# First product of a second MLP: seven products of 256 columns in place of eight, and an integer rounding

## The chip, the cores and the metric

The kernel runs on one core of a Trainium2 chip. The metric is the device time of one execution in microseconds (us). The engines are PE (matrix products), DVE, ACT and POOL (element work), and SP, which issues DMAs.

## What is computed

Attention in two stages over 8 batches of 576 positions, 8 heads of 64, gives x of 4608 rows and 512 columns. Two MLPs follow; the change concerns the second one.

```python
def _moe_ref(x, w_in, w_out):          # first MLP: 512 -> 2048 -> 512
    h = x @ w_in
    g = h * (1.0 / (1.0 + np.exp(-h)))
    return (g @ w_out).astype(np.float32)

def _moe2_ref(x, w_in, w_out):         # second MLP, same sizes
    h = x @ w_in
    g = h * np.cos(h)
    return (g @ w_out).astype(np.float32)
```

The weights arrive as 64-bit floats and are decoded in the kernel.

## The kernel before

Every operation is recorded by a planner (`Plan`, from line 81) together with what it reads and writes. The planner prices each one (`price`), works out due times backwards, simulates a list schedule several times, and then issues the operations in the order of the best schedule; so each engine has one fixed order, written down in advance, and all instructions carry the line at which the planner wraps a call, L196. `plan.due` sets a due time by hand, `plan.release` an earliest time. For PSUM, `region` (line 115) returns the whole bank, so operations on different columns of a bank are ordered one after the other. Operations recorded within `plan.either()` go to whichever of two engines the schedule finds first: `copy` to ACT or DVE, `combine` to DVE or POOL. `split(d, x)` (line 518) makes two parts of an fp32 tile, the rounded value and the rest, and `mm3` (line 502) multiplies split operands with three matmuls.

The first MLP runs over 256 steps (`first`, line 847) of 288 token columns and 128 of the 2048 hidden units: 6 matmuls into a bank of `hb`, then ACT, DVE and POOL work, then 12 into the four banks `acc`. Four pairs of batches follow each other, and the attention of the next pair runs between the steps. Results go to DRAM (`ydram`, and `ypart` for the first pair, which is computed in four parts). During the last pair, released at 380 us of the planner's time, `w2_unit` (line 565) prepares the second MLP's weights: load into one of two buffers `wd`, decode by way of `wy`, split into the same `wd`, store to `w2dram`; 32 units.

`change(top, [att], ...)` (line 1064) then closes the pool that holds attention's and the decoding's tiles and opens the tiles for y in its place, so y can be loaded once all of that is done. The second MLP goes over 9 blocks of 512 tokens and, in each, 16 chunks of 128 hidden units: 144 steps of `second` (line 923). A step is 12 matmuls of 512 columns into one of four banks in turn (`sb`, `mb`, `hb0`, `hb1`), then h x cos(h), then 12 matmuls of 512 columns into `acc`, due three steps later (`LAG`). The rounding of h/2pi is done by adding a large constant (`ROUND`) on ACT and subtracting it on DVE. All weights of the second MLP are loaded once and stay in `W`; `load_y` (line 905) loads and splits a block's input one block ahead, into two sets of buffers.

The functions that the change touches:

Of the kernel before, what the change touches and what calls it, by code (L numbers as in the profile page):

```python
# [25 lines left out]
ROUND = 12582912.0  # L26
# [54 lines left out]
class Plan:  # L81
# [73 lines left out]
    def price(self, engine, f, out, ins):  # L155
# [11 lines left out]
        if engine == self.DVE:  # L167
            fast = sbuf and f in ("tensor_copy", "tensor_scalar", "memset") and m == n
            if f == "scalar_tensor_tensor" and sbuf and ins[0].dtype == F32:
                return 67 + n / 0.53, 0  # L170
            return 67 + max(m, n) / (1.92 if fast else 0.96), 0
# [216 lines left out]
def attention_mlps_kernel(  # L388
# [24 lines left out]
    TB = 512  # L413
    NBLK = NT // TB
# [50 lines left out]
    w2dram = dram.tile([FC, 2, P, 2, 512], F32, name="w2dram")  # L465
# [13 lines left out]
    def late(name, dtype):  # L479

        return Late(name, W[0] if dtype == F32R else f32(W[0][:, 0]))
# [20 lines left out]
    def mm3(dst, lhs, rhs, first, last):  # L502

        T.matmul(dst, lhs[1], rhs[0], start=first, stop=False)
        T.matmul(dst, lhs[0], rhs[1], start=False, stop=False)
        T.matmul(dst, lhs[0], rhs[0], start=False, stop=last)
# [19 lines left out]
    late_wy = tiles(att, [P, WIDE], I32, "wy", 2)  # L526
# [38 lines left out]
    def w2_unit(c, i):  # L565
        if i == 0:
            src = w_in2[:, 2 * c * P : 2 * (c + 1) * P].rearrange("(k p) f -> p k f", p=P)
        else:
            src = w_out2[c * P : (c + 1) * P]
        DMA.dma_start(w2dram[c, i], f32(decode_parts(src)))  # L570

# [275 lines left out]
    def first(s):  # L847
# [28 lines left out]
        if end:  # L876
            t0 = pr * 2 * S + k0
# [9 lines left out]
    NS2 = NBLK * FC  # L887
    order = list(range(3, NBLK)) + [0, 1, 2]
    win, wout = {}, {}
    yt = {}  # L890
    banks = [sb, mb, hb[0], hb[1]]

    def lates(name, dtype, n):
        ts = [late(f"{name}{i}", dtype) for i in range(n)]
        return ts, ring(ts)

    ysts, yst = lates("yst", F32, 1)
    yads, yad = lates("yad", F32, 1)
    ys, yring = lates("y", F32R, 2 * KC)
    ns, nring = lates("n", F32, 2)  # L900
# [4 lines left out]
    def load_y(i, c):  # L905

        t0 = order[i] * TB
        st = yst()
        DMA.dma_start(st, ydram[c, :, t0 : t0 + TB])
        n = min(TB, 2 * S - t0)  # L910
        for part in ypart if n > 0 else ():
            ad = yad()
            DMA.dma_start(ad[:, :n], part[c, :, t0 : t0 + n])
            combine(st[:, :n], st[:, :n], ad[:, :n], ALU.add)
        yt[i, c] = yring()
        split(yt[i, c], st)

    def load_w2(c, base):
        win[c], wout[c] = W[base[0]], W[base[1]]
        DMA.dma_start(f32(win[c]), w2dram[c, 0])  # L920
        DMA.dma_start(f32(wout[c]), w2dram[c, 1])

    def second(s):

        i, fc = divmod(s, FC)
        h = banks[s % 4]
        w = win[fc]
        plan.due = due_second(s)
        for kc in range(KC):
            c = slice(kc * P, kc * P + P)  # L930
            y = yt[i, kc]
            mm3(h, (w[:, 0, c], w[:, 1, c]), (y[:, 0], y[:, 1]), kc == 0, kc == KC - 1)
        plan.due = None
# [12 lines left out]
        w = wout[fc]  # L946
        for t in range(4):
            plan.due = due_second(s + LAG)
            c = slice(t * P, t * P + P)
            mm3(acc[t], (g[:, 0, c], g[:, 1, c]), (w[:, 0], w[:, 1]), fc == 0, fc == FC - 1)  # L950
            plan.due = None
            if fc == FC - 1:
# [5 lines left out]
                r0 = order[i] * TB + t * P  # L958
                DMA.dma_start(out[r0 : r0 + P, :], o)
# [6 lines left out]
    def due_second(s):  # L966
        return due_first(NS) + 5540 * s
# [70 lines left out]
    for pr in range(NPAIR):  # L1038
# [25 lines left out]
    change(top, [att], "yp", "right", ysts + yads + ys)  # L1064
    change(mid, [a2p], "cp", "left", ns + rs_ + g2s + os_)
    for c in range(KC):
        load_y(0, c)
    for c in range(FC):
        if c < 4:
            load_w2(c, (FC + 2 * c, FC + 2 * c + 1))  # L1070
        elif c < 8:
            load_w2(c, (FC + 4 + c, FC + 8 + c))
        else:
            load_w2(c, (2 * (c - 8), 2 * (c - 8) + 1))
    for s in range(NS2):
        i, fc = divmod(s, FC)
        if fc == 0 and i + 1 < NBLK:
            for c in range(KC):
                load_y(i + 1, c)
        second(s)  # L1080
# [28 lines left out]
```

## Time and profile before

| | us |
|---|---|
| median of 3 runs | 1580.67 (1580.16 to 1581.14) |
| span of the profiled execution | 1579.2 |
| PE busy | 1554.3 |
| DVE / ACT / POOL busy | 1101.2 / 783.5 / 200.2 |
| DMA, mean over the span | 99 GB/s |

The profiled execution is one more run; its span goes from its first to its last instruction and is 1.5 us under the median of the timed runs. A record of PE lasts longer than the slot that the matmul takes, since matmuls are pipelined: rates are read from starts and counts, not from the mean length. PEld is the loading of the weights of a matmul.

### The profile page before, as it was taken

The page shows a single profiled execution, that of the slowest core. Times are in us where ns is not written, and L with a number is a line of the kernel's source. Part 1 is how long each engine was busy: PE and PEld are TensorE (multiplying, and loading weights), DVE is VectorE, ACT ScalarE, POOL GpSimd, SP SyncE. Part 2 cuts the span into 40 slices and gives each one's busy share as a digit, 9 for nine tenths or more (in the row PEclk, how much of TensorE's full clock was granted, in tenths as well). Part 3 has the DMA queues.
Part 4 walks back from the last instruction along what each step waited for, and adds up shares of the span by engine and source line. Part 5 has one row for each costly group of instructions (what it writes and reads, how often), then busy time and mean ns, then how long its engine had stood idle before and what let it go on. Part 6 is the DMA issues. An engine that isn't in the chain of part 4 may idle for free.

```text
span 1579.2 us, 26881 instructions
## 1 busy us (share of the span) xinstructions
PE 1554.3 (98%) x10344; PEld 1339.1 (85%) x10344; DVE 1101.2 (70%) x2031; ACT 783.5 (50%) x1549; POOL 200.2 (13%) x189
## 2 busy tenths in 40 slices
PE   9889999999999999999999999999999999999999
PEld 7678888999789988899988888888888888888887
DVE  5897666465787879775366767676766878676665
ACT  5876545344455565644344544444444444444443
POOL 0221111010112112120000010000100112121111
PEclk9899999999999999999999999999999999999999
DMA  9667475122775677552720101010010303010000
GB/s 248 178 221 206 124 151 136 51 46 51 165 230 184 182 175 195 193 196 83 257 99 7 47 1 54 1 54 1 27 48 20 95 19 94 21 61 0 20 9 27
DMA packets 217665, 156.96 MB, mean 99 GB/s; under 512 B 154048, under 2 KB 182720, under 8 KB 217536
## 3 DMA queue, kind: packets, MB, share of 16 engines
q1 hardware_dynamic: 217536, 155.24, 34.1%
q8 instruction: 81, 1.33, 0.4%
q14 instruction: 48, 0.39, 0.1%
HBM read 108.27 MB, written 46.92 MB: 98 GB/s over the span
## 4 chain that ended last, share of the span: by engine, by line
PE 86%; DVE 9%; DMA 2%; ACT 1%; issue 1%; SPq 0%; POOL 0%; DVEq 0%; ACTq 0%; POOLq 0%
PE acc L196 45%; PE hb L196 23%; PE sb L196 9%; PE mb L196 9%; DVE wy L196 2%; DVE big L196 1%; DVE w L196 1%; DVE wd L196 1%; DVE gf L196 1%; DMA wd<-in_moe_w_out 1%; DVE wde L196 1%; DVE rsb L196 1%; DVE g L196 0%; SPq L196 0%; DMA w2dram<-wd 0%
## 5 line engine op out<-in xcount | busy, mean ns | idle before, releaser
L196 PE MATMUL acc<-g,w 128*128 128x288 f32 x3072 | 470.1, 298 | 2.8 <-ACT ysb L196 2.1
L196 PE MATMUL acc<-w,g 128*128 128x512 f32 x1728 | 464.0, 389 | 0.8 <-DVE o L196 0.8
L196 PEld LDWEIGHTS acc<-g,w 128*128 128x128 f32 x3072 | 425.8, 188 | 28.9 <-issue 19.9
L196 PEld LDWEIGHTS acc<-w,g 128*128 128x128 f32 x1728 | 324.1, 188 | 69.2 <-DVE o L196 1.5
L196 PE MATMUL hb<-a,w 128*128 128x288 f32 x1536 | 263.8, 301 | 7.1 <-ACT a L196 2.9
L196 PEld LDWEIGHTS hb<-a,w 128*128 128x128 f32 x1536 | 222.6, 190 | 30.1 <-issue 14.9
L196 ACT ACTIVATE r<-r 128x512 f32<-128x512 f32 x144 | 91.0, 632 | 315.9 <-DVE r L196 315.5
L196 PE MATMUL hb<-y,w 128*128 128x512 f32 x864 | 239.2, 389 | 0.0
L196 PEld LDWEIGHTS hb<-y,w 128*128 128x128 f32 x864 | 162.1, 188 | 33.6
L196 ACT CAST g<-gf 128x288 fp32r<-128x288 f32 x223 | 96.2, 432 | 159.2 <-PE acc L196 125.6
L196 DVE SCALAR_TENSOR_TENSOR gf<-gf,hb 128x288 f32<-128x288 f32 x256 | 114.0, 447 | 55.0 <-ACT gf L196 53.6
L196 POOL TENSOR_TENSOR g<-gf,g 128x288 fp32r<-128x288 f32 x89 | 86.3, 970 | 508.2 <-ACT g L196 428.4
L196 ACT ACTIVATE gf<-hb 128x288 f32<-128x288 f32 x256 | 104.5, 411 | 87.9 <-PE hb L196 77.5
L196 DVE TENSOR_TENSOR g<-gf,g 128x288 fp32r<-128x288 f32 x167 | 78.1, 469 | 98.7 <-ACT g L196 97.1
L196 POOL TENSOR_TENSOR g<-r,g 128x512 fp32r<-128x512 f32 x44 | 57.1, 1298 | 591.1 <-ACT g L196 586.3
L196 DVE SCALAR_TENSOR_TENSOR r<-n,r 128x512 f32<-128x512 f32 x144 | 125.5, 871 | 2.8
L196 PE MATMUL sb<-y,w 128*128 128x512 f32 x432 | 121.6, 389 | 0.0
L196 PE MATMUL mb<-y,w 128*128 128x512 f32 x432 | 120.9, 389 | 0.0
L196 ACT ACTIVATE r<-r,half_pi 128x512 f32<-128x512 f32 x144 | 104.1, 723 | 4.1
L196 DVE TENSOR_TENSOR r<-r,hb 128x512 f32<-128x512 f32 x72 | 49.5, 687 | 74.9 <-ACT r L196 74.5
L196 PEld LDWEIGHTS mb<-y,w 128*128 128x128 f32 x432 | 80.9, 188 | 16.7
L196 PEld LDWEIGHTS sb<-y,w 128*128 128x128 f32 x432 | 81.0, 188 | 16.6
(189 smaller groups left out, 1576.4 us busy)
## 6 DMA issues: line engine op xcount, KB each, us to landing
w2dram<-wd SPq DMA_DIRECT2D x32, 512.0 KB, 3.3
w<-w2dram SPq DMA_DIRECT2D x32, 512.0 KB, 4.5
wd<-in_moe_w_in SPq DMA_DIRECT2D x24, 512.0 KB, 4.4
w<-w1dram SPq DMA_DIRECT2D x48, 256.0 KB, 3.4
wd<-in_moe_w_out SPq DMA_DIRECT2D x20, 512.0 KB, 4.2
ydram<-ysb SPq DMA_DIRECT2D x64, 144.0 KB, 2.2
yst<-ydram SPq DMA_DIRECT2D x36, 256.0 KB, 2.6
out<-o SPq DMA_DIRECT2D x36, 256.0 KB, 2.1
```

The source lines that it names most:

```text
L196: run = lambda: emit(*[real(x) for x in args], **{k: real(x) for k, x in kw.items()})
```

## The change

The first product of the second MLP is computed with Strassen's scheme: the two halves of a batch's tokens and the two halves of the 512 inputs and of the 2048 hidden units make a 2x2 by 2x2 product, for which seven products of combined operands stand in place of eight. A block is now 256 tokens of either half of the batches (columns t of `ydram` are rearranged to that end), a step covers two chunks of hidden units, `fp` and `fp + 8`, and there are 72 steps. A product is 2 chunks of inputs x 3 matmuls of 256 columns. It is accumulated in halves of two banks, X (`hb`) and Y (`mb`, `sb`), alternating by step; between the products two ACT copies and two DVE sums carry partial results from one half to another. The combined weights are made beforehand (`win2_unit`), stored in `w2s` and loaded anew for every block, 256 KB for each product, into a ring of 16 buffers; those of product 0 stay. The combined inputs are made in `load_y` (products 0 to 2) and during the last step of the block before (products 3 to 6). The second product is as before, with other due times. The rounding is done by letting ACT write 32-bit integers. A third buffer `wy` is added. One branch of the planner's price now looks at the last operand's type.

The core of the diff:

```diff
-    TB = 512
-    NBLK = NT // TB
+    TB = 256
+    NBLK = NT // (2 * TB)
+    FH = FC // 2
-    w2dram = dram.tile([FC, 2, P, 2, 512], F32, name="w2dram")
+    w2dram = dram.tile([FC, P, 2, 512], F32, name="w2dram")
+    w2s = dram.tile([2, 7, P, 4, 2, 2, P], F32, name="w2s")
-    late_wy = tiles(att, [P, WIDE], I32, "wy", 2)
+    late_wy = tiles(att, [P, WIDE], I32, "wy", 3)
+    def wout2_unit(c):
+        DMA.dma_start(w2dram[c], f32(decode_parts(w_out2[c * P : (c + 1) * P])))
+    def win2_unit(F, c):
+        def block(y, i, j):
+            f = (FH * i + 4 * F) * P
+            decode(w_in2[(c + 2 * j) * P : (c + 2 * j + 1) * P, 2 * f : 2 * (f + 4 * P)], y)
+        def put(y, prod):
+            flat = rings["wd"]().rearrange("p f t -> p (f t)")
+            d = flat.bitcast(F32R).rearrange("p (q t f) -> p t q f", q=4, t=2)
+            split(d, y.bitcast(F32).rearrange("p (q f) -> p q f", q=4))
+            DMA.dma_start(w2s[F, prod, :, :, c].rearrange("p q t f -> p q (t f)"), flat.bitcast(F32).rearrange("p (q x) -> p q x", q=4))
+        y = [rings["wy"]() for _ in range(3)]
+        v = [x.bitcast(F32) for x in y]
+        block(y[0], 1, 0)
+        block(y[1], 1, 1)
+        combine(v[2], v[0], v[1], ALU.add)
+        put(y[1], 6)
+        block(y[1], 0, 0)
+        put(y[1], 0)
+        put(y[2], 1)
+        combine(v[2], v[2], v[1], ALU.subtract)
+        combine(v[0], v[1], v[0], ALU.subtract)
+        put(y[2], 2)
+        put(y[0], 4)
+        block(y[1], 0, 1)
+        put(y[1], 3)
+        combine(v[1], v[1], v[2], ALU.subtract)
+        put(y[1], 5)
-    banks = [sb, mb, hb[0], hb[1]]
+    X, Y = hb, [mb, sb]
+    raws, raw = lates("raw", F32, 10, TB)
+    ys, _ = lates("y", F32R, 12, TB)
+    yring = ring(ys + [as_y(x) for x in halves[0:2] + halves[26:32]])
+    held = halves[2:4] + halves[20:26]
+    uring = ring(halves[4:16] + halves[16:20])
+    AHEAD_Y = 3
         n = nring()
-        A.activation(n, h, AF.Copy, scale=INV_2PI / WEIGHT, bias=ROUND)
-        V.tensor_scalar(n, n, ROUND, None, op0=ALU.subtract)
+        A.activation(n, h, AF.Copy, scale=INV_2PI / WEIGHT)
-            plan.due = due_second(s + LAG)
+            plan.due = due_second(s + (2.1 if fc >= FH else 1.6))
+    def second(s):
+        i, fp = divmod(s, FH)
+        x, y = X[s % 2], Y[s % 2]
+        x1, x2, y1, y2 = x[:, :TB], x[:, TB:], y[:, :TB], y[:, TB:]
+        ws = [held[fp]] + [uring() for _ in range(6)]
+        ws = [as_w(ws[0]) if i else load_unit(ws[0], fp, 0)] + [load_unit(w, fp, j) for j, w in enumerate(ws) if j]
+        def product(prod, dst, start, due):
+            plan.due = due_second(s + due)
+            for c in range(2):
+                b = yt[i, prod, c]
+                w = ws[prod]
+                mm3(dst, (w[:, c, 0], w[:, c, 1]), (b[:, 0], b[:, 1]), start and c == 0, c == 1, skip_group_check=True)
+            plan.due = None
+            if fp == FH - 1 and i + 1 < NBLK and prod + AHEAD_Y < 7:
+                later[i + 1](prod + AHEAD_Y)
+        m5 = m5ring()
+        product(0, x1, True, 0)
+        product(1, x2, False, 0.1)
+        A.copy(y1, x1)
+        A.copy(m5, x2)
+        product(2, y1, False, 0.35)
+        product(3, x1, False, 0.45)
+        V.tensor_tensor(x2, y1, m5, ALU.add)
+        product(4, y1, False, 0.6)
+        product(5, x2, False, 0.7)
+        V.tensor_tensor(y2, y1, m5, ALU.add)
+        half_second(s, fp, x)
+        product(6, y1, False, 0.95)
+        half_second(s, fp + FH, y)
-        return due_first(NS) + 5540 * s
+        return due_first(NS) + 10480 * s
-            for c in range(FC):
-                for i in range(2):
-                    w2_unit(c, i)
+            for F in range(2):
+                for c in range(2):
+                    win2_unit(F, c)
+                for c in range(4 * F, 4 * F + 4):
+                    wout2_unit(c)
+                    wout2_unit(c + FH)
-    change(top, [att], "yp", "right", ysts + yads + ys)
+    change(top, [att], "yp", "right", raws + yads + m5s + ys)
+    load_y(0)
+    for prod in range(AHEAD_Y, 7):
+        later[0](prod)
```

## Rows read from the trace of the kernel before

**Rows 1.** The page's part 1: busy us, share of the span, instructions, for PE.

```profile
PE 1554.3 (98%) x10344; PEld 1339.1 (85%) x10344; DVE 1101.2 (70%) x2031; ACT 783.5 (50%) x1549; POOL 200.2 (13%) x189
```

**Rows 2.** Busy time by stretch: PE, PEld, DVE, ACT, POOL (count), granted clock, DMA share, GB/s.

```profile
560.00:720.00 160.00, 157.42 (x1377) 141.34 (x1376) 123.70 (x244) 88.69 (x204) 26.74 (x26) 1.00 0.65 191
720.00:800.00 80.00, 80.00 (x575) 78.19 (x574) 36.91 (x81) 32.05 (x69) 0.81 (x1) 1.00 0.55 178
800.00:1560.00 760.00, 759.23 (x3348) 627.75 (x3347) 537.33 (x892) 348.60 (x564) 90.15 (x75) 1.00 0.10 32
```

**Rows 3.** The chain that ended last: start, length, what.

```profile
820.13 2.27 PE hb L196 x10
841.89 2.27 PE hb L196 x10
```

**Rows 4.** Busy time by stretch, where PE runs 288-column matmuls alone.

```profile
720.00:780.00 60.00, 60.00 (x455) 60.00 (x454) 28.27 (x64) 23.34 (x53) 0.81 (x1) 1.00 0.48 156
```

**Rows 5.** Instructions in order of time, PEld: start, length, engine, operation, count.

```profile
555.38 0.30 PEld L196 LDWEIGHTS acc<-g,w 128*128 128x128 f32 x2
...
555.75 0.19 PEld L196 LDWEIGHTS acc<-g,w 128*128 128x128 f32 x1
```

**Rows 6.** Groups by shape, 800 to 1560 us: count, busy us, mean ns, idle before.

```profile
L196 DVE SCALAR_TENSOR_TENSOR r<-n,r 128x512 f32<-128x512 f32 x141 | 123.4, 875 | 2.7
...
L196 ACT ACTIVATE r<-r,half_pi 128x512 f32<-128x512 f32 x141 | 102.0, 723 | 4.1
L196 ACT ACTIVATE r<-r 128x512 f32<-128x512 f32 x140 | 88.5, 632 | 309.5 <-DVE r L196 309.0
...
L196 DVE TENSOR_TENSOR g<-r,g 128x512 fp32r<-128x512 f32 x97 | 68.4, 705 | 2.2
L196 ACT CAST g<-r 128x512 fp32r<-128x512 f32 x104 | 64.4, 620 | 28.6 <-DVE r L196 26.7 <-POOL yst L196 1.6
L196 DVE TENSOR_SCALAR n<-n 128x512 f32<-128x512 f32 x140 | 63.0, 450 | 32.6 <-ACT n L196 32.4
L196 DVE TENSOR_SCALAR r<-r 128x512 f32<-128x512 f32 x140 | 60.4, 431 | 4.1
...
L196 DVE SCALAR_TENSOR_TENSOR r<-n,hb 128x512 f32<-128x512 f32 x71 | 48.8, 687 | 3.5
...
L196 ACT ACTIVATE n<-hb 128x512 f32<-128x512 f32 x71 | 42.2, 594 | 25.9 <-PE hb L196 25.5
```

**Rows 7.** The page's part 5 and its longer view: 288-column operations on DVE and ACT.

```profile
L196 DVE TENSOR_TENSOR g<-gf,g 128x288 fp32r<-128x288 f32 x167 | 78.1, 469 | 98.7 <-ACT g L196 97.1
...
L196 ACT ACTIVATE ysb<-acc 128x288 f32<-128x288 f32 x107 | 41.4, 411 | 24.4 <-PE acc L196 16.5 <-DMA ypart<-ysb 5.7 <-DMA ydram<-ysb 1.8
```

**Rows 8.** A 256 KB load (KB, us to landing), and the busiest DMA stretch.

```profile
w<-w1dram SPq DMA_DIRECT2D x48, 256.0 KB, 3.4
...
760.00:800.00 40.00, 40.00 (x273) 38.19 (x272) 16.48 (x35) 15.88 (x33) 0.00 (x0) 1.00 0.80 269
```

**Rows 9.** Tile `wd`, 410 to 710: ns min/median/max, first and last start; DMA to landing.

```profile
L196 ACT ACTIVATE wd<-wd x32: 659/675/697, 419.5 to 690.1; 128x512 int32<-128x512 uint32 x32
...
L196 DVE SCALAR_TENSOR_TENSOR wy<-wy,wd x32: 673/692/1640, 422.0 to 695.1; 128x512 int32<-128x512 int32 x32
...
L196 SPq DMA_DIRECT2D w2dram<-wd x32: 319/326/1448, 427.7 to 700.7; - x32
...
w2dram<-wd SPq DMA_DIRECT2D x32, 512.0 KB, 3.3
...
wd<-in_moe_w_in SPq DMA_DIRECT2D x24, 512.0 KB, 4.4
```

**Rows 10.** Tile `yst` 700 to 760, and PE in order of time.

```profile
L196 SPq DMA_DIRECT2D yst<-ydram x9: 319/320/427, 708.0 to 748.8; - x9
...
783.38 0.39 PE L196 MATMUL sb<-y,w 128*128 128x512 f32 x1
```

**Rows 11.** PE in order of time at the end.

```profile
1561.75 13.54 PE L196 MATMUL acc<-w,g 128*128 128x512 f32 x59
```

More of the change, by code (lines that the diff above doesn't have):

```diff
@@ L25 @@
 TWO_PI_LO = 2.0 * math.pi - 6.28125
-ROUND = 12582912.0
 DOWN = 2.0**-111
@@ L500, in attention_mlps_kernel, with mm3 @@
     pbds = [const.tile([P, H // 2, 2 * NP], F32, name=f"pbd{i}") for i in range(2)]
[L502 to L506, printed above, removed]
+    def mm3(dst, lhs, rhs, first, last, **kw):
+        T.matmul(dst, lhs[1], rhs[0], start=first, stop=False, **kw)
+        T.matmul(dst, lhs[0], rhs[1], start=False, stop=False, **kw)
+        T.matmul(dst, lhs[0], rhs[0], start=False, stop=last, **kw)
     def copy(dst, src):
@@ L876, in first @@
         if end:
-            t0 = pr * 2 * S + k0
+            t0 = k0 // HALF % 2 * (2 * S if part else NT) // 2 + (2 * pr + k0 // S) * HALF
             dst = ypart[part - 1] if part else ydram
@@ L903, in attention_mlps_kernel @@
     os_, oring = lates("o", F32, 2)
-    def load_y(i, c):
-        t0 = order[i] * TB
[L908 to L933, printed above, removed]
+    halves = [W[FC + kc * 4 + s][:, i] for s in range(4) for kc in range(2) for i in range(2)]
+    halves += [W[FC + 8 + kc * 4 + s][:, i] for s in range(4) for kc in range(2) for i in range(2)]
@@ new lines, in attention_mlps_kernel, with load_y, load, put @@
+    as_y = lambda x: x.rearrange("p (t n) -> p t n", t=2)
+    as_w = lambda x: x.rearrange("p (k t f) -> p k t f", k=2, t=2)
+    yring = ring(ys + [as_y(x) for x in halves[0:2] + halves[26:32]])
+    held = halves[2:4] + halves[20:26]
+    uring = ring(halves[4:16] + halves[16:20])
+    AHEAD_Y = 3
+    later = {}
+    def load_y(i):
+        t0 = order[i] * TB
+        n = min(TB, S - t0)
+        def load(kc, h):
+            st = raw()
+            DMA.dma_start(st, ydram[kc, :, h * NT // 2 + t0 : h * NT // 2 + t0 + TB])
+            for part in ypart if n > 0 else ():
+                ad = yad()
+                DMA.dma_start(ad[:, :n], part[kc, :, h * S + t0 : h * S + t0 + n])
+                combine(st[:, :n], st[:, :n], ad[:, :n], ALU.add)
+            return st
+        b11 = [load(c, 0) for c in range(2)]
+        b12 = [load(c, 1) for c in range(2)]
+        b21 = [load(c + 2, 0) for c in range(2)]
+        b22 = [load(c + 2, 1) for c in range(2)]
+        t2 = [raw() for c in range(2)]
+        def put(prod):
+            for c in range(2):
+                x, minus = {
+                    0: (b11, None),
+                    1: (b11, (b12, b11)),
+                    2: (t2, (b22, b11)),
+                    3: (b21, None),
+                    4: (b12, (b22, b12)),
+                    5: (b22, None),
+                    6: (b21, (b21, t2)),
+                }[prod]
+                if minus:
+                    combine(x[c], minus[0][c], minus[1][c], ALU.subtract)
+                yt[i, prod, c] = yring()
+                split(yt[i, prod, c], x[c])
+        for prod in range(AHEAD_Y):
+            put(prod)
+        later[i] = put
@@ L957, in second @@
                     A.activation(o, acc[t], AF.Copy, scale=WEIGHT**-2)
-                r0 = order[i] * TB + t * P
-                DMA.dma_start(out[r0 : r0 + P, :], o)
+                p0 = order[i] * TB + t % 2 * P
+                cuts = [p0] + list(range(p0 // HALF * HALF + HALF, p0 + P, HALF)) + [p0 + P]
+                for a, b in zip(cuts, cuts[1:]):
+                    r0 = a // HALF * S + t // 2 * HALF + a % HALF
+                    DMA.dma_start(out[r0 : r0 + b - a, :], o[a - p0 : b - p0])
+    def second(s):
[27 more added lines that the diff above has]
+        half_second(s, fp + FH, y)
     def due_first(s):
```

65 lines of the change are left out of this document (32 added, 33 removed).

## The prediction

> **What bounds the kernel now.** I read the page's busy shares first, then the busy time by stretch, then the chain of waits, then groups by shape. PE is busy 1554.3 us of a span of 1579.2, 98% [rows 1]. From 800 to 1560 us, the second MLP, PE is busy 759.23 of 760 us at full granted clock (1.00, the 2.4 GHz level), while DVE works 537 us, ACT 349, POOL 90 and the DMA engines move 32 GB/s [rows 2]. So in this half only what PE has to stream counts. The chain says the same: one and the same piece, ten matmuls into `hb`, returns every 21.76 us (820.13, 841.89) [rows 3]. That is four steps of `second`, 96 matmuls of 512 columns: 226.7 ns each. Two old steps, which the new `second` does in one, take 10.88 us, and 144 old steps 783.4 us. The first MLP is different: between 560 and 720 us PE loses 2.6 of 160 us and DVE is busy 77%, but from 720 to 800 us DVE is at 46%, ACT at 40%, POOL at 1% [rows 2].
>
> **The price of a 256-column matmul.** The trace has none; two lengths of the same kind of operand bound it. 512 columns cost 226.7 ns, 13.4 over 512/2.4. In 720 to 780 us 455 matmul records, all of 288 columns, touch a window that PE fills [rows 4]; without the two in flight at its ends one starts every 60/453 = 132.5 ns, 12.5 over 288/2.4. The line through both points gives 118.9 ns at 256. A floor could lie above it: every matmul here has its own weight load, and halving the columns doubles the loads per column. The nearest rows: two weight loads of 128x128 together last 0.30 us, though one alone lasts 0.19, so the second began 0.11 us behind the first [rows 5]. A load can thus follow a load at 110 ns, under 118.9. From above the price is held by the 132.5 ns of 288 columns, from below by that 110. I take 119 because the slope is carried by two plentiful rows and the load rate lies below it.
>
> The Trainium skill, "TensorE: Matmul & The Clock Gate", section "Back-to-back issue gap", gives N/2.4 + 2.5 ns for a lone stream, hence 215.8 ns at 512 columns and 109.2 at 256; by that the second MLP would lose 42.7 us. The trace disagrees at 512 (226.7 ns), so the measured line is used.
>
> **The change part by part.**
> 1. *First product of the second MLP.* Removed per pair of steps: 24 matmuls of 512. Added: 7 products x 2 chunks x 3 terms = 42 of 256. The second product stays at 24 of 512. New step: 24 x 226.7 + 42 x 119 = 5441 + 4998 = 10439 ns against 10882; 443 ns saved, 72 times: **-31.9 us**. With 110 ns it is -59.1, with 132.5 it is +8.9.
> 2. *Exchanges inside a step.* Products share halves of a bank, and the planner's `region` knows PSUM by whole banks, so ACT's two copies wait for the second product, product 2 for the copy into `y1` and product 3 for both; DVE's sum into `x2` waits for product 3, product 4 for that sum; the sum into `y2` waits for product 4 and product 6 for it. No row shows a 256-column copy out of PSUM. 288 columns cost ACT 411 ns and 512 cost 594, so some 385; DVE's two-operand sums cost 469 at 288 and 705 at 512, so some 435 [rows 6, 7]. A matmul's record outlives its slot by 0.16 us (389 against 227 ns). PE without other work would stand about 0.16 + 2 x 0.385 = 0.93 us after product 1, and 0.16 + 0.435 = 0.6 us after product 3; product 5 (0.71 us) covers the third. If ACT is inside its 723 ns operation or DVE inside its 875 ns one, the two gaps reach 1.65 and 1.5 us. The cover is the 24 matmuls of the second product, 5.4 us per step, which belong to earlier steps and are ready: a half's chain n, two subtractions, clamp, abs, sine, product, split is 0.59+0.69+0.88+0.43+0.63+0.72+0.69+0.62+0.71 = 6.0 us (0.69 twice, for the two DVE operations that read the bank) [rows 6], and they are due 1.6 and 2.1 steps (16.7 and 21.9 us) behind their step's start. So 0 to 0.2 us per step; I take 0.03, **+2 us**. Without the cover it would be 1.5 us x 72 = 110 us.
> 3. *Integer rounding.* Removes 144 DVE operations of 450 ns [rows 6], 65 us of DVE work, none of it on the chain: no time of its own. ACT now writes int32; 594 ns with an fp32 output and 675 for an int32 one in the weight decoding [rows 9] are its bounds, and ACT has room for both.
> 4. *What DVE and ACT do now.* DVE has 537/760 x 10.88 = 7.7 us per pair of steps. Minus 0.9 (rounding), plus two sums 0.9, plus the y splits (per block 14 of 256 columns and 8 differences at some 0.43, for 4 splits of 512 at 0.71: 6.6 us, 0.8 per step): 8.5 of 10.44. ACT: 5.0 + 0.8 + 0.4 = 6.2. Neither becomes the bound. But differences and splits of products 3 to 6 of the next block have buffers only in a block's last step: 12 sums and 8 casts, some 5 us on DVE if all go there, beside the evictions of `acc`. That step asks 11 to 13 us of DVE; POOL, 12% busy [rows 2], can take part, and the slack of the following steps pays back. Bounds 0 and 3 us at each of 8 borders, I take 0.5: **+4 us**.
> 5. *Streamed weights.* Each step loads 6 units of 256 KB (7 in the first block): 1.57 MB in 10.44 us, 151 GB/s, plus 25 for y and out. SP issues 6 more DMAs per step at 0.3 us [rows 9]. Queued on SP behind a load that waits for its buffer are the y loads and outputs; 16 buffers are 2.7 steps, 28 us, against 3.4 us to landing for a 256 KB load of today [rows 8]. The queues gave 269 GB/s from 760 to 800 us and 191 over 560 to 720 us [rows 2, 8], with PE full in the first of these. Price 0; if the cover went, each late unit would cost its 3.4 us.
> 6. *Preparing the combined weights.* It stands in the last pair of the first MLP, in two `wd` buffers. Today 32 units run from the first load, 4.4 us ahead of the first decoding operation at 419.5, to the last store, issued at 700.7 and 3.3 us long: 415 to 704, 289 us [rows 9]. A unit holds its buffer for load 4.4, decoding 3.3 (five operations of 0.5 to 0.7), split 1.3, store 3.3 = 12.3 us by its own operations [rows 6, 9]. Now there are 16 such, 16 that only load and decode (7.7) and 28 that only split and store (4.6): 449 us of holding for 394. 289 x 1.14 = 330 us: the last store lands at about **745 us**. The y buffers open only then; today the y loads begin at 708 and the first product that reads y at 783.38 [rows 10]. From 745 the first splits need a load (2.7 us) and some 1.5 us of work on half idle engines: cover of over 30 us, price 0. The extra work before that, 12 splits and 16 differences, is some 20 us of DVE or more of POOL, and 7 of ACT, where PE already loses 2.6 us in 160: 0 to 6, I take **+2 us**.
> 7. *Start and end.* At the start the last second products of the first MLP (36 x 0.13 = 4.8 us) and two steps of Strassen products (10 us) cover the first chain (6 us of exchanges and products, then 6 us): 0 to 3, take **+1**. At the end today 59 matmuls run without a gap from 1561.75 to the last [rows 11]; the old order keeps three steps of 2.7 us in hand. The new one has after the last product 12 matmuls of the step before and 12 of its own first half, while the last half's chain takes 6.0 us and the first half's ends some 5 us after: a gap of about **+2.7 us** (0 to 4).
>
> **The sum.** -31.9 + 2 + 4 + 2 + 1 + 2.7 = -20.2 us. The profiled execution's span of 1579.2 becomes 1559; the median shown is 1.5 us more than the span, so 1580.7 - 20.2 = **1560.5 us**. I say 1560.
>
> **The rivals.**
> *A. The exchanges are not covered (slower).* Place: before products 2 to 4 of every step. The order on PE is written down in advance; where ACT or DVE is later than planned, PE waits with ready work behind the waiting matmul. For it: four exchanges per step on engines that queue 0.7 to 0.9 us operations. Against it: today's waits of the same kind (PE's bank to ACT's `n`, chain, PE) cost under 1 us in 760. It decides from 20.2/72 = 0.28 us per step; half of the gaps uncovered (0.76 us) gives 1560 + 55 = 1615, a third of that 1578.
> The Trainium skill, "PSUM — Partial Sum Buffer", section "PSUM bank collisions raise a hardware error", says that two engines must not be in one bank at once, even on different columns. No row of before shows a bank used by halves; by that rule the copies cannot start while product 1 runs beside them, which is the order costed above.
> *B. The preparation ends late (slower).* From 775 us on each us of delay is one of the total; that needs 360 us for the 289 of today, a factor of 1.25 where I have 1.14. For it: 60 uses of two buffers instead of 32, and the y tiles tie a unit's decodes and splits in series. At a factor of 1.4 it ends at 820, 45 us late: 1605.
> *C. A 256-column matmul costs what 288 columns cost.* 132.5 ns: +8.9 instead of -31.9, 1601 us. Against it the 0.11 us between loads.
> *D. It does what it says and gains nothing.* Losses of 0.1 to 0.3 us per step and 2 us per border add up to the gain: 1577 to 1584.
> *E. The weight stream becomes the bound*, if the queues gave less than 176 GB/s beside this work: 1590 or more. Rows of 191 and 269 speak against it.
>
> **How the numbers follow.** Forecast (1548 to 1577) 0.75; D 0.08; A 0.08; B 0.05; C 0.03; E 0.01. Faster by over 0.2% (3.2 us, about what a measurement of this kernel can tell from no change) 0.75, the same 0.08, slower 0.17. Low end: 117 ns per short matmul (-42) with 6 us of the losses, and the end gap: 1548. High end: through D, 1584. Left out: 0.17 above, some 0.02 below.
>
> **What would show it.** Starts of 256-column matmuls 119 ns apart within a product; 24 + 42 matmuls every 10.4 to 10.5 us, granted clock still 1.00; PE idle under 0.1 us per step, named to ACT `y`/`m5` or DVE `x2` if there is more; the last `w2s` store near 745 us and the first y-reading product still near 783; an idle piece of 2 to 3 us before the last 12 matmuls. I am wrong if the step is over 10.8 us, if short matmuls are over 125 ns apart in a full stretch, or if the second MLP begins after 795 us.

## The result and the profile after

The changed kernel takes 1592.5 us (median of 4 runs, 1590.6 to 1596.1) against 1580.9 for the kernel before beside it: a ratio of 1.0072, interval 1.0056 to 1.0088. It is slower by 11.6 us, where 20 us less were forecast; 1592.5 lies above the range, which ended at 1584.

The page's parts 1, 2 and 5 of the changed kernel (its operations carry line L195):

```profile
span 1591.8 us, 31263 instructions
...
PE 1547.5 (97%) x11642; PEld 1379.5 (87%) x11642; DVE 1135.9 (71%) x2114; ACT 855.4 (54%) x1801; POOL 308.1 (19%) x326
...
PEclk9889999999999999999999999999999999999999
...
L195 PE MATMUL acc<-w,g 128*128 128x512 f32 x1728 | 469.4, 395 | 3.9 <-POOL g L195 2.2
```

Against [rows 1], PE is busy 7 us less and the span is 12.6 us longer, so PE stands idle 44.3 us instead of 24.9. POOL has 108 us more. The idle time is the first thing to see: the work left PE, and PE waits.

Where the time is follows from four marks in each trace: the starts of the first MLP's 16th and 112th step, its last matmul, and PE's end.

| us | before | after | difference |
|---|---|---|---|
| 16th step of the first MLP starts | 118.9 | 128.8 | +9.9 |
| 112th step starts | 392.6 | 400.4 | +7.8 |
| last matmul of the first MLP | 795.5 | 817.3 | +21.8 |
| end of PE | 1575.3 | 1587.8 | +12.5 |

(These marks are matmul starts of the trace, the last row excepted; 12 matmuls into `acc` make a step, and steps are counted from 0. The expectations below call the 16th step the 32nd and the 112th the 128th; the times they give are those of the table.)

So the second MLP is 9.3 us shorter, not 31.9 less some losses, and the first MLP, of which the change touches only the decoding and preparation of weights, is 21.8 us longer. The two MLPs run into each other: 66 matmuls of the second (7.85 us at the prices below) stand before the first one's last matmul, where it was 24 (5.44 us), so 2.4 of the 21.8 us are work that comes earlier. Busy time by stretch, first the kernel before, then the changed one (PE, PEld, DVE, ACT, POOL, granted clock, DMA share, GB/s):

```profile
40.00:130.00 90.00, 81.09 (x741) 66.93 (x741) 83.85 (x160) 69.99 (x152) 22.76 (x20) 0.91 0.65 202
390.00:795.00 405.00, 398.75 (x3356) 364.16 (x3356) 294.18 (x587) 210.92 (x475) 58.78 (x58) 1.00 0.63 186
```

```profile
40.00:130.00 90.00, 78.98 (x727) 63.58 (x722) 80.40 (x152) 67.54 (x145) 26.79 (x19) 0.85 0.61 191
390.00:795.00 405.00, 391.16 (x3339) 355.87 (x3338) 302.47 (x588) 211.37 (x489) 101.69 (x94) 1.00 0.64 184
820.00:1580.00 760.00, 751.14 (x4638) 667.70 (x4637) 560.60 (x969) 421.32 (x802) 153.54 (x180) 1.00 0.57 178
```

At the start, 40 to 130 us, PE is idle 2.1 us more, and its granted clock is 0.85 of full speed instead of 0.91. It fell to the 1.2 GHz level at 47.4, 95.2 and 125.9 us, where PE had just stood idle for 2.3, 1.3 and 1.8 us; over these 90 us that is some 5 us of full speed less. From 390 to 795 us PE is idle 7.6 us more, with 8 us more on DVE and 43 on POOL. In the second MLP PE is idle 8.9 us of 760, where it was idle 0.8 [rows 2].

The second MLP closer, PE in order of time. Starts give the rates: six 256-column matmuls from 1063.49 to 1064.21 are 120 ns each; seven of 512 columns from 1064.21 to 1065.82 are 230, twelve from 1067.62 to 1070.36 are 228:

```profile
1063.49 0.88 PE L195 MATMUL hb<-y,w 128*128 128x256 f32 x6
1064.21 1.78 PE L195 MATMUL acc<-w,g 128*128 128x512 f32 x7
1065.82 0.52 PE L195 MATMUL hb<-y,w 128*128 128x256 f32 x3
...
1067.62 2.91 PE L195 MATMUL acc<-w,g 128*128 128x512 f32 x12
1070.36 0.75 PE L195 MATMUL mb<-w,w 128*128 128x256 f32 x5
```

Over all starts that follow a matmul without a stall, 256 columns take 119.0 ns and 512 take 231.6, against 226.7 before. The second is new. In a row of 512-column matmuls the first cost 234, 235, 229, 232, 231 ns, from the sixth on 226 to 227 again, and behind the first 256-column matmul after such a row the next one starts 113 ns later rather than 120. So the first five cost 27 to 28 ns more in all, and the first 256 behind the row gives 7 back. Time between starts beyond these prices is called a stall below: 18.1 us in the second MLP, more than PE's idle time, since a record outlasts its slot. Some 13 of them stand in the first two of a block's eight steps.

And the longest stall of the second MLP, at a border between blocks:

```profile
1236.38 3.47 POOL L195 TENSOR_TENSOR raw<-raw,raw 128x256 f32<-128x256 f32 x4
1238.22 0.40 ACT L195 CAST y<-raw 128x256 fp32r<-128x256 f32 x1 [1.55 <-POOL raw L195]
1238.53 0.62 ACT L195 ACTIVATE r<-r 128x512 f32<-128x512 f32 x1
1239.06 0.39 ACT L195 CAST y<-raw 128x256 fp32r<-128x256 f32 x1
1239.35 0.36 ACT L195 COPY mb<-hb 128x256 f32<-128x256 f32 x1
1239.77 0.98 PE L195 MATMUL mb<-w,w 128*128 128x256 f32 x6 [1.61 <-ACT mb L195]
```

ACT's queue holds a cast of y that needs a sum from POOL. POOL takes 0.87 us for each and is late; ACT stands idle 1.55 us; behind the cast stands the exchange copy `mb<-hb`, and behind that PE's product 2, which waits 1.61 us.

### The profile page after: what moved, and what is told of

It reads as the page before. It is cut to its first block, busy times and chain, and to the rows that moved or that the text cites. A ratio compares the mean times of both kernels' runs of the same rounds, so it can differ in the third digit from the quotient of the medians.

```text
span 1591.8 us, 31263 instructions
## 1 busy us (share of the span) xinstructions
PE 1547.5 (97%) x11642; PEld 1379.5 (87%) x11642; DVE 1135.9 (71%) x2114; ACT 855.4 (54%) x1801; POOL 308.1 (19%) x326
## 4 chain that ended last, share of the span: by engine, by line
PE 76%; DVE 11%; DMA 5%; ACT 3%; issue 2%; POOL 2%; SPq 1%; DVEq 0%; POOLq 0%; ACTq 0%
PE acc L195 41%; PE hb L195 21%; PE mb L195 7%; PE sb L195 7%; DVE r L195 2%; DMA yad<-ypart 1%; DVE wy L195 1%; DVE wd L195 1%; DMA wd<-in_moe_w_in 1%; SPq L195 1%; DVE g L195 1%; DVE w L195 1%; DVE big L195 1%; DVE y L195 1%; DVE raw L195 1%
## 5 line engine op out<-in xcount | busy, mean ns | idle before, releaser
L195 PE MATMUL acc<-w,g 128*128 128x512 f32 x1728 | 469.4, 395 | 3.9 <-POOL g L195 2.2
L195 PE MATMUL acc<-g,w 128*128 128x288 f32 x3072 | 469.9, 298 | 3.1 <-POOL g L195 2.2
L195 PEld LDWEIGHTS acc<-g,w 128*128 128x128 f32 x3072 | 426.1, 189 | 29.3 <-issue 20.5
L195 PEld LDWEIGHTS acc<-w,g 128*128 128x128 f32 x1728 | 301.0, 189 | 50.9 <-POOL g L195 3.8
L195 PE MATMUL hb<-a,w 128*128 128x288 f32 x1536 | 264.2, 303 | 13.5 <-DVE gf L195 5.4
L195 PEld LDWEIGHTS hb<-a,w 128*128 128x128 f32 x1536 | 223.8, 192 | 35.7 <-issue 13.2
L195 POOL TENSOR_TENSOR g<-gf,g 128x288 fp32r<-128x288 f32 x91 | 92.1, 1014 | 522.6 <-ACT g L195 437.7
L195 ACT CAST g<-gf 128x288 fp32r<-128x288 f32 x225 | 97.3, 433 | 175.4 <-PE acc L195 129.8
L195 PE MATMUL hb<-y,w 128*128 128x256 f32 x1056 | 166.1, 282 | 0.2 <-DVE hb L195 0.2
L195 PEld LDWEIGHTS hb<-y,w 128*128 128x128 f32 x1056 | 150.3, 190 | 10.4 <-DVE hb L195 0.4
L195 DVE SCALAR_TENSOR_TENSOR gf<-gf,hb 128x288 f32<-128x288 f32 x256 | 114.2, 448 | 50.8 <-ACT gf L195 49.1
L195 DVE TENSOR_TENSOR g<-gf,g 128x288 fp32r<-128x288 f32 x165 | 80.4, 488 | 97.3 <-ACT g L195 96.2
L195 ACT ACTIVATE gf<-hb 128x288 f32<-128x288 f32 x256 | 104.6, 410 | 67.5 <-PE hb L195 60.9
L195 ACT CAST g<-r 128x512 fp32r<-128x512 f32 x141 | 87.7, 622 | 72.3 <-DVE r L195 72.0
L195 DVE TENSOR_TENSOR g<-r,g 128x512 fp32r<-128x512 f32 x130 | 92.6, 712 | 46.4 <-ACT g L195 45.6
L195 ACT ACTIVATE r<-r 128x512 f32<-128x512 f32 x144 | 90.7, 630 | 42.2 <-DVE r L195 41.8
L195 DVE SCALAR_TENSOR_TENSOR r<-n,r 128x512 f32<-128x512 int32 x144 | 108.6, 754 | 3.5
L195 PE MATMUL hb<-w,w 128*128 128x256 f32 x672 | 109.9, 282 | 0.1
L195 ACT ACTIVATE r<-r,half_pi 128x512 f32<-128x512 f32 x144 | 104.2, 724 | 3.2
L195 PEld LDWEIGHTS hb<-w,w 128*128 128x128 f32 x672 | 97.9, 190 | 8.5 <-DVE hb L195 0.7
L195 ACT ACTIVATE n<-hb 128x512 int32<-128x512 f32 x72 | 43.0, 597 | 83.6 <-PE hb L195 83.5
L195 POOL TENSOR_TENSOR y<-raw,y 128x256 fp32r<-128x256 f32 x47 | 41.0, 882 | 169.6 <-ACT y L195 119.1
```

Source lines behind the costliest of these rows:

```text
L195: run = lambda: emit(*[real(x) for x in args], **{k: real(x) for k, x in kw.items()})
```

## The experiments

**The start: which part of the change delays the first MLP before any preparation?** Theory: the third `wy` buffer, which the decoding at the start uses as well, reorders the start. Rival: the planner's search is tipped by any change.

`e1_boot_two_wy`, the changed kernel:

```diff
-    buffers(late_wd + early_wd, late_wy)
+    buffers(late_wd + early_wd, late_wy[:2])
```

> The changed kernel, but the decoding at the start uses two wy buffers as before; the third is used from the preparation on. The first MLP of the changed kernel ran 9 to 10 us behind from its 32nd step on (128.8 us against 118.9). If the third buffer reorders the start: 32nd step back at about 119 us, total about 1583. If the shift comes from the planner's search, which a change anywhere in the program can tip: 32nd step anywhere between 115 and 130, and total within 1580 to 1597 without relation to the buffer.

Measured 1581.5 us, ratio 0.9992 (0.9980 to 1.0003). The 16th step starts at 119.5, and the 112th at 391.1.

`e2_before_wy3`, the kernel before:

```diff
-    late_wy = tiles(att, [P, WIDE], I32, "wy", 2)
+    late_wy = tiles(att, [P, WIDE], I32, "wy", 3)
```

> The kernel before, with three wy buffers and nothing else. If the third buffer is what makes the start late: 32nd step of the first MLP at about 128 us and total about 1589. If it is the search that another program tips: some other shift, or none, total 1578 to 1590.

Measured 1589.0 us, ratio 1.0041 (1.0025 to 1.0056); 16th step at 127.3. Both sides agree: one more buffer, without a further change, costs 6.6 us by the medians (interval 4.0 to 8.9), and 8.9 us at the 112th step of its trace. First `e1_boot_two_wy`, then `e2_before_wy3`:

```profile
40.00:130.00 90.00, 81.14 (x741) 67.11 (x742) 82.71 (x161) 69.41 (x151) 22.50 (x18) 0.91 0.66 199
```

```profile
40.00:130.00 90.00, 79.48 (x714) 63.60 (x705) 80.46 (x152) 65.62 (x141) 24.40 (x20) 0.85 0.55 180
```

This holds in every run of this document: with three buffers at the start (five kernels) the 16th step starts at 127.3 to 128.8 us and the clock from 40 to 130 us is 0.85 to 0.87; with two (thirteen kernels) it starts at 117.6 to 120.6, and the clock is 0.89 to 0.94. So the buffer does it, and not a search that any change tips. Which decoding step passes which other in the planned order was not followed further.

`e3_rounding`, the integer rounding and its price in the kernel before:

```diff
-        A.activation(n, h, AF.Copy, scale=INV_2PI / WEIGHT, bias=ROUND)
-        V.tensor_scalar(n, n, ROUND, None, op0=ALU.subtract)
+        A.activation(n, h, AF.Copy, scale=INV_2PI / WEIGHT)
```

> The kernel before with the integer rounding (and the price that goes with it) alone. PE fills the second MLP, so 65 us less of DVE work give nothing there: second MLP still 226.7 ns for each matmul and 779 to 780 us from the last matmul of the first MLP to the end. Total 1580.7 plus whatever the planner's other order does to the first MLP: 0 if orders are stable, up to 10 us either way if the search is tipped by any change.

Measured 1585.3 us, ratio 1.0013 (1.0002 to 1.0024). Matmuls stay at 226.8 ns; DVE is busy 1050.4 us instead of 1101.2, and that gives nothing, as PE was the bound. The last matmul of the first MLP comes at 798.1, 2.6 later, and from there to the end it takes 781.7 instead of 779.8: an order tipped by a small change is worth 2 to 5 us here.

**The second MLP: what makes the 512-column matmuls slow, and what the stalls?**

`e4_no_stream` takes the streaming of the weights away after the first block:

```diff
-[load_unit(w, fp, j) for j, w in enumerate(ws) if j]
+[as_w(w) if i else load_unit(w, fp, j) for j, w in enumerate(ws) if j]
```

> The changed kernel, with the combined weights loaded in the first block alone; later blocks multiply by what lies in the ring (this leaves out the reloading of products 1 to 6). 512-column matmuls of the changed kernel start 231.6 ns apart on average instead of 226.7. If the 150 GB/s beside them slow them: 226.7 again and 8 us less in the second MLP. If it is the mixture with 256-column matmuls: 231 to 232 again, and under 3 us less. Stalls at block borders: unchanged if they come from the work on y, gone if loads come late.

Measured 1589.2 us; DMA falls from 178 to 45 GB/s, but 512 columns stay at 231.7 ns and the stalls go from 18.1 only to 15.8 us. The stream is not the cause of the price, and makes at most 2.3 us of the stalls.

```profile
820.00:1580.00 760.00, 751.73 (x4646) 670.58 (x4645) 562.56 (x972) 425.09 (x811) 135.96 (x169) 1.00 0.15 45
```

`e7_halves` mixes lengths in the kernel before, without Strassen's scheme; each 512-column matmul of the first product becomes two:

```diff
-            mm3(h, (w[:, 0, c], w[:, 1, c]), (y[:, 0], y[:, 1]), kc == 0, kc == KC - 1)
+            mm3(h[:, :256], (w[:, 0, c], w[:, 1, c]), (y[:, 0, :256], y[:, 1, :256]), kc == 0, kc == KC - 1)
+            # and a second loop over kc for the columns from 256 on
```

> The kernel before, where each 512-column matmul of the second MLP's first product is made as two of 256 columns: same products, no exchanges, no streamed weights, no other work on y. It measures the price of short matmuls and of mixing them with 512-column ones by itself. If mixing costs as in the changed kernel: 256 columns start 119 ns apart, 512 columns 231 to 232, a step of two chunks 24 x 231.6 + 48 x 119 = 11.27 us, second MLP some 28 us longer (total about 1609). If 512 columns return to 226.7 ns, the mixture is not the cause: 11.15 us, total about 1600.

Measured 1631.0 us: 256 columns at 119.0 ns, 512 at 231.8, without any stream or exchange. PE in order of time; four of 512 columns from 1002.58 to 1003.51 are 232 ns each, twenty of 256 from 1000.20 to 1002.58 are 119:

```profile
1000.20 2.55 PE L196 MATMUL mb<-y,w 128*128 128x256 f32 x20
1002.58 1.09 PE L196 MATMUL acc<-w,g 128*128 128x512 f32 x4
1003.51 0.40 PE L196 MATMUL mb<-y,w 128*128 128x256 f32 x2
```

So the mixture makes the price. The trace of the kernel before shows it too, where its two MLPs run into each other: eight matmuls of 512 columns from 792.21 to 794.06, between 288-column ones, are 231 ns each, and of the row that starts at 795.64 the first eight cost 229 to 235 ns, the others 226 to 227:

```profile
792.21 2.02 PE L196 MATMUL mb<-y,w 128*128 128x512 f32 x8
794.06 1.74 PE L196 MATMUL acc<-g,w 128*128 128x288 f32 x12
795.64 2.69 PE L196 MATMUL hb<-y,w 128*128 128x512 f32 x11
```

The total of `e7_halves` came out 22 us above the 1609 expected: 15 us of stalls (1.3 before), nearly all where a block's second products wait until the outputs of the block before have left `acc`, and 7 us more in the first MLP, whose preparation is that of the kernel before. So an order can cost that much without exchanges, stream or new preparation.

`e8_group` issues the 12 matmuls of a half's second product as one block, on top of `e1_boot_two_wy`:

```diff
+            with plan.together():
+                for t in range(4):
+                    mm3(acc[t], ...)
```

> The changed kernel with two wy buffers at the start, and the 12 matmuls of a half's second product issued as one block. After a row of 256-column matmuls the first five of 512 columns cost 229 to 235 ns, then 227. If that toll is paid per change of length: mean of the 512-column starts 229 or less, 3 to 5 us less in the second MLP. Against it: PE can fill its waits only in pieces of 2.7 us, which can add stalls to the 16.5 us of e1_boot_two_wy. If the toll is not per change: 231.6 again.

Measured 1595.8 us, ratio 1.0099 (1.0080 to 1.0118). 512 columns fall to 229.1 (229 or less was expected), as a toll on each change of length would have it, but the stalls rise from 16.5 to 36.3 us, as the argument against it feared: PE has no small pieces left to fill its waits with. How much of the rise is that, and how much the new order, is not shown. The net is a loss.

`e6_y_no_sums` leaves the eight subtractions that combine y out:

```diff
-                if minus:
-                    combine(x[c], minus[0][c], minus[1][c], ALU.subtract)
                 # and product 2 takes b22 as it is
```

> The changed kernel without the eight subtractions per block that combine y (the products get uncombined halves; this leaves out the combining of y). The stalls of PE in the second MLP, some 17 us, stand around the block borders, where ACT's copies between banks queue behind casts of y that wait for POOL's sums. If that is the cause: stalls fall to under 8 us, total about 1583. If the exchanges inside every step are late: stalls unchanged, total 1590 or more.

Measured 1581.7 us against 1581.0 (ratio 1.0002, 0.9987 to 1.0016), but of the 10.3 us by which its span is under the changed kernel's, 6.4 stand in the first MLP (last matmul at 810.9 instead of 817.3); stalls are 14.2 us, not under 8. These sums alone are not the cause.

`e9_y_once`, on top of `e1_boot_two_wy`: every block uses the first block's y, and no y is loaded or made for the others:

```diff
+        if i:
+            yt[i, prod, c] = yt[0, prod, c]    # for all products
+            return
```

> The changed kernel with two wy buffers at the start, and all blocks multiply the y of the first block (this leaves out loading, adding, combining and splitting y for the other eight). If the stalls of PE in the second MLP (16.5 us in e1_boot_two_wy) come from the work on y at the borders, in whose queues the exchanges wait: under 4 us of stalls, second MLP about 13 us shorter, total about 1568. If they come from the exchanges themselves: over 12 us of stalls remain.

Measured 1565.8 us; stalls 2.9 us instead of 16.5, the second MLP 13.4 us shorter. The exchanges of 72 steps are covered; the work on y beside them uncovers those at the borders. Three kernels then asked which part of that work does it, on top of `e1_boot_two_wy`.

`e11_y_ahead`, room for all products of the next block:

```diff
-    AHEAD_Y = 3
+    AHEAD_Y = 7    # one y tile more, seven halves moved from uring to yring
```

> The changed kernel with two wy buffers at the start, and room for all 28 y operands of two blocks (one more tile, and seven halves taken from the ring of streamed weights, which falls from 16 to 9): all products of the next block are prepared during the block, none has to wait for its last step. If the stalls at the borders (16.5 us in e1_boot_two_wy) come from the burst in the last step: under 8 us, total about 1572. If the amount of work on y or POOL's lateness makes them, wherever it stands: 12 to 20 us. If nine buffers are too few for the weights: stalls in every step, total above 1585.

Measured 1586.5 us, ratio 1.0029 (1.0015 to 1.0042), stalls 21.8. But the plan did not use the room: in the block from 1146 to 1232 us no work on y starts before 1212.

```profile
L195 ACT CAST y<-raw x10: 389/406/408, 1212.2 to 1229.9; 128x256 fp32r<-128x256 f32 x10
```

The other blocks are alike: of ACT's 32 us of casts of y 28 fall into a block's last two steps and the first of the next. So the run says nothing on the burst at a block's end, and whether work on y that is spread out would cost less stays open. The nine buffers were not too few: among the waits of PE's weight loads in the second MLP there is none for a DMA.

`e13_exch_either`, the exchange copies on ACT or DVE:

```diff
-        A.copy(y1, x1)
-        A.copy(m5, x2)
+        copy(y1, x1)
+        copy(m5, x2)
```

> The changed kernel with two wy buffers at the start, and the two exchange copies on ACT or DVE, as the planner chooses. If ACT's queue alone makes the exchanges late: stalls fall by the 9 us that PE's weight loads into mb and sb waited for ACT. If the planner does not see the lateness it cannot avoid it: 14 to 18 us as before.

Measured 1582.5 us, stalls 23.9: no gain either. Only four of the 144 copies went to DVE, three of the 72 into `m5` (here `m`) among them:

```profile
L195 ACT COPY m<-hb x69: 352/375/384, 790.6 to 1556.0; 128x256 f32<-128x256 f32 x69
```

So the run does not tell what these copies would gain on DVE. That the planner does not know of the lateness, and so has no ground to move them, fits this but is not shown. What the run does show is that four moved copies, with the order that came with them, can change the stalls by 7.4 us.

`e12_y_dve`, the sums of y on DVE alone:

```diff
-                    combine(x[c], minus[0][c], minus[1][c], ALU.subtract)
+                    V.tensor_tensor(x[c], minus[0][c], minus[1][c], ALU.subtract)
```

(and the same for the addition of the parts)

> The changed kernel with two wy buffers at the start, and the sums that combine y and add the parts on DVE alone instead of DVE or POOL. If ACT's casts of y wait for POOL's sums (0.75 to 0.87 us each and up to 6 us late by their loads), and the exchange copies behind them: stalls fall from 16.5 to under 9 us. If it is DVE's load: 20 us or more.

Measured 1570.3 us, ratio 0.9929 (0.9910 to 0.9949); stalls 9.1 us. Who PE's weight loads waited for (us in total, times, longest), `e1_boot_two_wy`, then `e12_y_dve`, then `e9_y_once`:

```profile
PEld mb L195 <- ACT mb L195: 6.8, 8, 2.0
PEld acc L195 <- DVE g L195: 2.9, 6, 0.8
PEld acc L195 <- POOL g L195: 2.5, 5, 1.2
```

```profile
PEld sb L195 <- DVE hb L195: 2.6, 6, 0.6
PEld acc L195 <- POOL g L195: 2.1, 4, 0.9
PEld mb L195 <- ACT mb L195: 1.7, 5, 0.7
```

```profile
PEld mb L195 <- ACT mb L195: 1.5, 6, 0.6
```

The wait for ACT's copy into `mb` goes from 6.8 to 1.7 us, what is left with no work on y at all is 1.5. DVE was 74% busy in this stretch and became 76%; POOL fell from 139 to 70 us. Of the 13.3 us between the spans of the two profiled executions 7.7 lie in the second MLP; the other 5.6 lie in the first, which this edit does not touch.

After `e13_exch_either` a fall of 7.4 us in the stalls could be the luck of one order. Over all runs it is not: in the nine kernels with the changed product that make y for every block and may put its sums on POOL, the stalls are 14.2 to 36.3 us; in the four that have them on DVE (the other three follow) they are 5.6 to 9.8. They go with POOL's time on `raw`, the buffers that hold y before its rounding, from 820 to 1560 us: 127 us in `e1_boot_two_wy`, 95 in `e6_y_no_sums`, 59 in this run, none in the next.

`e14_y_split_dve` puts the second half of y's splits on DVE too:

```diff
-                split(yt[i, prod, c], x[c])
+                d = yt[i, prod, c]
+                copy(d[:, 0], x[c])
+                V.tensor_tensor(d[:, 1], x[c], f32(d[:, 0]), ALU.subtract)
```

> The kernel of e12_y_dve with the second half of every split of y on DVE too, so POOL has no part in y. If POOL's operations make the remaining 9.1 us of stalls: 3 to 6 us, second MLP about 4 us shorter, total about 1566. If DVE's load becomes the limit (28 sums and 112 splits more a run): stalls of 12 us or more, total above 1573.

Measured 1568.2 us, ratio 0.9915 (0.9895 to 0.9934); stalls 5.6 us, in the range expected, while its first MLP ended 4.6 us later than that of `e12_y_dve`.

**The preparation.** `e5_light_prep` decodes, splits in place and stores without combining:

```diff
+            y = rings["wy"]()
+            flat = decode(w_in2[...], y)
+            # split into the same wd, one or two stores; no sums, no further wd
```

> The changed kernel with the weight preparation cut to what it was before: each block of w_in is decoded, split in place and stored to the places of one or two products (this leaves out the combining of the weights: 16 sums, 12 splits and 28 further uses of the two wd buffers; the 28 stores stay). If the preparation is what delayed the first MLP by 12 us between 400 and 817 us: its last matmul at about 805 instead of 817, total about 1580. If the delay comes from a tipped order of the plan: between 810 and 825, total 1585 to 1600. Last store of the preparation near 720 instead of 780 us.

Measured 1588.3 us, with three `wy` buffers at the start as in the changed kernel. From the 112th step to the last 407.6 us, against 416.9 with the full preparation and 402.9 before; last store at 736 us instead of 776. So the stretch is 9.3 us shorter, but its start came 3.0 us later (403.4), and the last matmul (811.0) and the total fell into the ranges given for a tipped order. The run does not decide between the two.

`e10_early_prep` releases the preparation earlier, on top of `e1_boot_two_wy`:

```diff
-    LATER = 380e3
+    LATER = 230e3
```

> The changed kernel with two wy buffers at the start, and the weight preparation released at 230 instead of 380 us of the planner's time, into the stretch from about 240 to 400 us where DVE is at 45 to 65%. If the preparation costs the first MLP by crowding DVE and the two wd buffers after 400 us: from the 128th to the last step 403 to 408 us instead of 416, total about 1572. If any preparation costs PE the same wherever it stands: 1580 to 1583.

Measured 1583.0 us, ratio 1.0010 (1.0000 to 1.0020). From the 112th step on it takes 408.4 us, at the edge of what was hoped, but from the 80th to the 112th 91.8 instead of 85.2, and the total is that of the second case: the cost moved with the work.

`e15_prep_dve`, on top of `e12_y_dve`: the preparation's sums and the second halves of its splits on DVE:

```diff
-        combine(v[2], v[0], v[1], ALU.add)
+        V.tensor_tensor(v[2], v[0], v[1], ALU.add)    # and the other three, and the split in put
```

> The kernel of e12_y_dve with the sums and splits of the weight preparation on DVE alone. The stretch from the first MLP's 128th step to its last takes 414 us in e12_y_dve and 403 in the kernel before. If POOL's late results make that: 405 to 409, total about 1563. If DVE's load makes it: 416 or more, total 1572 or more.

Measured 1567.7 us, ratio 0.9916 (0.9898 to 0.9934); 409.8 us from the 112th step on, against 414.2: better, but between the two ranges given, as is the total. Stalls are 9.8 us. `e16_both_dve` joins it with `e14_y_split_dve`.

> The kernels of e14_y_split_dve and e15_prep_dve together: POOL has no part in y nor in the weight preparation. If the two causes add up: first MLP from its 128th step to its last about 410 us, stalls of the second MLP about 5.6 us, total about 1563. If each new order only moves the losses: 1566 to 1572.

Measured **1563.5 us, ratio 0.9876 (0.9850 to 0.9901)**; stalls 5.6 us, 410.4 us from the 112th step on. The version beats both kernels.

```profile
390.00:795.00 405.00, 395.23 (x3340) 360.26 (x3339) 313.37 (x611) 216.57 (x496) 69.95 (x65) 1.00 0.65 190
830.00:1550.00 720.00, 718.28 (x4474) 643.94 (x4473) 553.19 (x1086) 410.62 (x789) 8.24 (x6) 1.00 0.57 178
```

PE is idle 9.8 us in the first of these stretches (13.8 in the changed kernel, 6.3 before) and 1.7 in the second.

How far the preparation itself costs the first MLP is settled only between bounds. From the 112th step to the last, kernels with the old preparation took 402.0, 402.9, 403.1 and (`e7_halves`) 410.5 us; the changed kernel and the nine others with the full new one on DVE or POOL and its release unmoved 410.7 to 416.9; with its sums on DVE alone 409.8 and 410.4. Of each time of a changed kernel 2.4 us are matmuls of the second MLP that come earlier. Taking POOL out of the preparation gave 4.4 us (414.2 to 409.8) and 5.0 (415.4 to 410.4). What remains over the 403 of before, some 5 us, is the further work and the luck of the order, in shares that no run here separates: `e7_halves` lost 7 us to its order alone.

## Why the prediction was wrong

*The price of a short matmul* (first step) was right: 119.0 ns for 118.9 by the line, as [rows 4] and the 226.7 ns had it (120 inside a row; the first ones behind 512 columns pull the mean down). The load rate of [rows 5] did not bind. *The second product "stays at 24 of 512"* was wrong in its price: 231.6 for 226.7, 24 x 4.9 x 72 = **+8.5 us** that the sum did not have. Both rows that I fitted came from stretches of one length only; a mixture stood in no row, and I gave it no bound. The trace had one, from 783 to 797 us, with rows of 512 columns at 228 to 236 ns behind 288; it was there to be read. The Trainium skill's 109 and 216 ns ("TensorE: Matmul & The Clock Gate", "Back-to-back issue gap") were still further off the measured 119.0 and 231.6.

*Exchanges and borders* (steps 2 and 4) were put at +2 and +4. Stalls were 18.1 us for 1.3 before, **+16.8**. The mechanism named for rival A, a copy late on its engine and PE waiting behind it, is the one in the rows, but not its place: inside a block the cover of 24 matmuls held, as step 2 said, and at the borders it failed. Step 4 counted DVE's time and let "POOL take part" as a relief. POOL was the larger part of the cause: its sums took 0.87 us, a cast on ACT waited for them, and the exchange stood behind the cast. Without POOL in y the stalls are 5.6 us (`e14_y_split_dve`), without any work on y 2.9 (`e9_y_once`). I had asked who is queued behind the new waits for SP, and not for ACT. Step 7's +1 at the start did not come: from 804.41, the first product that reads y, to 817.3 PE runs without a stall. Nor did its end gap of 2.7 us; the last 50 matmuls, in order of time:

```profile
1575.65 6.46 PE L195 MATMUL acc<-w,g 128*128 128x512 f32 x27
1582.26 5.50 PE L195 MATMUL acc<-w,g 128*128 128x512 f32 x23 [0.15 <-DVE g L195]
```

They ran with 0.15 us of idle time, as the 59 of [rows 11] ran with none.

*Integer rounding* was put at nothing, and its work gave nothing; `e3_rounding` took 2.9 us more, with another order. *The stream* (step 5) was put at nothing; without it, in `e4_no_stream`, the stalls fall by 2.3 us, no more than a new order moves them.

*The preparation* (step 6) was put at +2 beside a cover of 30 us. Its last store came at 776 us, not 745; it began 8 us later and took 359 us where it took 289, a factor of 1.24, nearer B's 1.25 than my 1.14. The first product that reads y came at 804.4, past the 795 that I had named as a sign of being wrong; but PE did not stand waiting for it, since the first MLP ended later as well. The cost was the other one, in the first MLP: +14.0 us from the 112th step to the last, less the 2.4 that are second-MLP matmuls, **+11.6 us**. Of these the step had the mechanism (DVE and POOL work where PE already loses time) and a sixth of the size; its upper bound was 6. How much of them is the preparation and how much the luck of the order stays open, within the bounds above.

*What the prediction left out altogether* is the third `wy` buffer at the start, **+7.8 us** at the 112th step (`e1_boot_two_wy`, `e2_before_wy3`). The diff line was quoted, and the buffers' use at the start stands in the kernel; I read it as belonging to the preparation.

Together: -31.9 + 8.5 + 16.8 + 11.6 + 7.8 = +12.8 us. PE's end moved by 12.5; the 0.3 between them is not assigned. Of the rivals A came nearest, and the chance of 0.17 for slower was too low: four losses of moderate size, two in places with small entries in the sum and two in places with none, added up.

## What to carry to other kernels

A reduction of work on the bounding engine is worth what the engine in front of each new wait can still deliver in time: follow each new wait back through the queue of the engine that ends it, and ask which slower engine that queue itself waits for. Giving work to an idle slow engine is no relief where a fast in-order engine then waits for it; here 69 us taken from POOL and given to a DVE at 74% brought 7.4 us of stalls. When a buffer is added for one stage, look for every other stage that turns the same ring, and with a planned order time that part alone.

## What was not expected of the hardware

A 512-column matmul costs 226.7 ns among its like and 229 to 235 ns for the first five behind 256-column ones (231.6 and 231.8 on average in two kernels that share nothing else new; behind 288 columns, in the kernel before, the first eight of a row take 229 to 235), while 256 columns cost 119 to 120 and 113 to 117 right behind 512. Why the price rises for several matmuls and then falls back was not found. After idle pieces of PE of 1.3 to 2.3 us the granted clock fell to the 1.2 GHz level: 0.85 for 0.91 over the start, some 5 us of full speed in 90.
